# Plain tiles 2 and 3 written out in order with attention stages at points, w_out blocks kept, weight steps spaced wider

## The chip, the core and the metric

The kernel runs on one core of a Trainium2 chip. The metric is the device time of one execution in microseconds (us). A core has TensorE (matmuls; PE in the profile, with PEld for its weight loads), VectorE (DVE), ScalarE (ACT), GpSimd (POOL), SyncE (SP), which here issues all DMAs, and 16 DMA engines.

## What is computed

Attention with keys and values pooled over 8 positions, then a first FFN (leaky ReLU), then an RMS norm and a second FFN (gated by SiLU), in float32 (the weights come as float64 and are converted by bit operations):

```python
# q, k, v: (8, 8, 576, 64); 4608 tokens of 512 features
k_p = k.reshape(B, H, 72, 8, D).mean(axis=3); v_p = v.reshape(B, H, 72, 8, D).mean(axis=3)
scores = q @ k_p.T / sqrt(D)
attn = exp(scores - max(scores)); attn = attn / (attn.sum(-1) + 1e-09)
x = (attn @ v_p).transpose(0, 2, 1, 3).reshape(4608, 512)
h = x @ w_in                              # w_in 512 x 2048
x = maximum(0.01 * h, h) @ w_out          # w_out 2048 x 512
xn = x / sqrt(mean(x * x) + 1e-06) * rms_g
g = xn @ w_gate; val = xn @ w_val         # 512 x 1536 each
out = (g * sigmoid(g) * val) @ w_out2     # w_out2 1536 x 512
```

## The kernel before

**Numbers.** Every float32 operand is kept as two parts, HI and LO, and a product is three matmuls (`TERMS`): HI x HI, HI x LO, LO x HI. Splitting an operand takes a copy on ScalarE (the high part) and a subtraction on VectorE or GpSimd (the low part).

**Attention** goes by batch b (0 to 7) and by tiles t (0 to 4) of 128 queries. Steps of one tile: `t` transposes the queries (TensorE rows `qt`), `s` makes the scores in two halves (`sc`) and the softmax (VectorE maximum and subtraction, ScalarE exponential, VectorE sum, reciprocal, product), `x` transposes the result (`xt`, and a small rest `xr`) and splits it. Per batch, `kp` and `vp` pool keys and values on GpSimd, `kt` transposes the keys, and `av` multiplies with the values (`av0` after tile 1, `av1` after tile 4). The result goes to the token tiles `xhl` in SBUF, or from token 1536 on to `x_dram`.

**First FFN, plain tiles.** The first 1536 tokens are three plain tiles of 512 (`PLAIN` = 3; here tile 0, 1, 2). For each of 16 blocks f of the hidden layer, `h_unit` multiplies with a block of w_in (128 hidden units, 12 matmuls, rows `h`), ScalarE and VectorE make the activation's parts, and two blocks later `y_unit` multiplies with the block of w_out (12 matmuls into four banks, rows `y`). In tile 0 the first 8 blocks are done in halves of 256 columns, because its last 256 tokens come later. Attention's steps (`seq`) are cut by shares into lists for the three tiles (`by_tile`, `border`) and put between the units. This part is ordered by the compiler's scheduler, which simulates times; `own(...)` keeps some instructions in the order of the code.

**First FFN, pairs.** The other 3072 tokens are three pairs of tiles (pair 0, 1, 2), computed with seven block products instead of eight (`Quad`: p1 to p7, rows `xh`, `yh`, `wh` on operands `xa`, `T`, `xb`, `ah`). A pair has 8 quads; the second half z=1 of its output is multiplied afterwards with all 16 blocks of w_out again (`y_part`, rows `o<-ug,wo`). Its operands are written to DRAM by `operand_steps` in tile 2 (GpSimd rebuilds the weights, VectorE forms sums, ScalarE and GpSimd split them, SyncE stores them) and come back by `load_a` into ten slots; w_out comes back by `load_o` into four slots. `token_steps` forms the token sums T1 to T4 of a pair. From the first pair on every engine keeps the order of the code. After each product (a **point**) `tick` issues a part of what is left of attention (`late_attention`: query tiles from (4, 2) on, `RATE` = 7 points apart) and, when attention has ended, one step of `side_steps`, which prepares the second FFN's weights in the same way: per unit a load, a conversion, sums, split, store, with a unit every 6 (gate and value) or 4 points (w_out2).

**Second FFN.** Five more pairs with six g/v quads each; `norm_steps` computes their RMS norm in points of the pair before.

## Time and profile before

| | us |
|---|---|
| three runs | 1942.01, 1946.44, 1946.67 |
| median | 1946.44 |
| profiled execution, time | 1941.65 |
| profiled execution, span | 1939.9 |
| TensorE busy | 1782.7 |
| its weight loads busy | 1498.6 |
| VectorE, ScalarE, GpSimd busy | 967.2, 734.0, 697.4 |

The mean granted clock of TensorE is 0.963 of full speed. How to read the rows below: a row of the table of stretches has the stretch (us from the span's start), its length, the busy time and the count of instructions of each engine, then TensorE's granted clock (1.00 is 2.4 GHz, 0.50 is 1.2 GHz), the share of time in which the DMA engines were busy, and GB/s. A row of the timeline has start, length, engine, line, operation, output and inputs, size, and in brackets the idle time before it with what ended it; matmuls overlap, so the distance of two starts tells more than a length. A row of waits has who waited for whom, us in all, how often, and the longest. A row of groups has busy time and mean length.

### The profile page before, as it was taken

To read this page: it belongs to the slowest core of one execution; us is meant where nothing else is said; L and a number is where in the kernel's file an instruction comes from. 1 tells how busy PE (TensorE), PEld (TensorE's weight loads), DVE (VectorE), ACT (ScalarE), POOL (GpSimd) and SP (SyncE) were. 2 spreads that over 40 slices of the span, in tenths; PEclk is the share of its full clock that TensorE was granted. 3 is DMA by queue.
4 is the path that set the end of the run, shared out by engine and by line. 5 is a ranking of instruction groups with operands and counts; after the bars stand their busy time and mean duration, and the time that the engine had idled before them with its cause. 6 is when DMAs were issued, how large, how long until landed. Compare 5 with 4: busy or idle time off the path is not lost. (4 is left out here: it accounts for less than half of the span.)

```text
span 1939.9 us, 24263 instructions
## 1 busy us (share of the span) xinstructions
PE 1782.7 (92%) x8452; PEld 1498.6 (77%) x8452; DVE 967.2 (50%) x1622; ACT 734.0 (38%) x1566; POOL 697.4 (36%) x792
## 2 busy tenths in 40 slices
...
GB/s 266 303 158 100 26 74 58 93 311 256 206 207 224 233 126 300 345 348 253 334 269 342 186 246 195 209 233 291 252 270 210 195 230 275 249 274 205 194 206 103
DMA packets 222345, 429.43 MB, mean 221 GB/s; under 512 B 60176, under 2 KB 114448, under 8 KB 221712
## 3 DMA queue, kind: packets, MB, share of 16 engines
...
## 5 line engine op out<-in xcount | busy, mean ns | idle before, releaser
L1282 PE MATMUL o<-wo,u 128*128 128x512 f32 x1296 | 315.2, 391 | 2.8 <-DMA wo<-wo 2.7
L1282 PEld LDWEIGHTS o<-wo,u 128*128 128x128 f32 x1296 | 242.2, 188 | 52.2 <-DMA wo<-wo 4.3
L1262 PE MATMUL o<-ug,wo 128*128 128x512 f32 x576 | 150.7, 413 | 19.4 <-DMA wo<-wo 8.6
L665 PE MATMUL h<-xhl,w_i 128*128 128x512 f32 (+1 forms) x672 | 155.9, 380 | 2.3 <-ACT g L100 1.9
L701 PE MATMUL y<-ghl,w_o 128*128 128x256 f32 (+1 forms) x768 | 152.0, 343 | 3.0 <-ACT ye L714 1.8
L1262 PE MATMUL o<-u,wo 128*128 128x512 f32 x576 | 148.1, 396 | 0.0
L1262 PEld LDWEIGHTS o<-ug,wo 128*128 128x128 f32 x576 | 111.1, 198 | 47.1 <-ACT oe L1269 9.2
L97 POOL TENSOR_TENSOR u<-e2g,u 128x512 fp32r<-128x512 f32 (+1 forms) x25 | 29.5, 1182 | 310.6 <-ACT u L94 310.6
L665 PEld LDWEIGHTS h<-xhl,w_i 128*128 128x128 f32 x672 | 120.2, 201 | 23.5 <-ACT g L100 2.9
L701 PEld LDWEIGHTS y<-ghl,w_o 128*128 128x128 f32 x768 | 120.8, 191 | 18.5 <-ACT ye L714 2.1
L1262 PEld LDWEIGHTS o<-u,wo 128*128 128x128 f32 x576 | 107.8, 190 | 21.8
L1173 POOL TENSOR_TENSOR u<-gu,u 128x512 fp32r<-128x512 f32 x42 | 56.2, 1337 | 168.9 <-ACT gu L100 168.8
L1152 PE MATMUL xh<-xa,ah 128*128 128x512 f32 x288 | 78.3, 409 | 15.0 <-ACT e1h L1196 15.0
L1152 PE MATMUL yh<-T,ah 128*128 128x512 f32 x288 | 79.4, 413 | 7.0 <-DVE e6h L1127 4.7
L1152 PE MATMUL yg<-T,ag 128*128 128x512 f32 (+1 forms) x360 | 84.1, 369 | 0.0
L1152 PE MATMUL yv<-T,av 128*128 128x512 f32 (+1 forms) x360 | 83.9, 368 | 0.0
L1152 PE MATMUL xg<-xa,ag 128*128 128x512 f32 (+1 forms) x360 | 83.8, 368 | 0.0
L1152 PE MATMUL xv<-xa,av 128*128 128x512 f32 (+1 forms) x360 | 83.8, 368 | 0.0
L231 POOL TENSOR_TENSOR v<-v 128x256 f32<-128x256 f32 (+2 forms) x84 | 56.4, 675 | 57.8 <-DMA v<-in_v_dram 54.2
L1152 PEld LDWEIGHTS xh<-xa,ah 128*128 128x128 f32 x288 | 54.8, 195 | 27.3 <-ACT e1h L1196 16.5
L1152 PEld LDWEIGHTS yg<-T,ag 128*128 128x128 f32 x360 | 66.0, 188 | 9.9 <-DVE e1v L1127 0.6
L1152 PEld LDWEIGHTS yv<-T,av 128*128 128x128 f32 x360 | 66.2, 188 | 9.5
...
## 6 DMA issues: line engine op xcount, KB each, us to landing
...
```

The source lines that it names most:

```text
L97: lo_eng.tensor_tensor(out=lo, in0=src, in1=hi.bitcast(F32), op=ALU.subtract)
L231: nc.gpsimd.tensor_tensor(out=x[:, :n], in0=x[:, :n], in1=x[:, n:2 * n], op=ALU.add)
L665: nc.tensor.matmul(pt, w[:, sp, c * P:(c + 1) * P], x[:, mp, c, :], start=c == 0 and i == 0, stop=c == n_k - 1 and i == 2,)
L701: nc.tensor.matmul(pt, w[:, sp, m * P:(m + 1) * P], g[:, mp, a - c0:a - c0 + n], start=ydone[j, a] == 1 and i == 0 and m % per_bank == 0, ...
L1152: nc.tensor.matmul(pt, wt[:, a, c, sp, :], xt[:, mp, :], start=start and c == 0 and i == 0, stop=c == 1 and i == 2, skip_group_check=not s ...
L1173: eng.tensor_tensor(out=t[:, LO, :], in0=g, in1=t[:, HI, :].bitcast(F32), op=ALU.subtract)
L1262: nc.tensor.matmul(pt, w[:, sp, m * P:(m + 1) * P], u[:, mp, :], start=f == 0 and i == 0, stop=f == F1 - 1 and i == 2,)
L1282: nc.tensor.matmul(pt, u[:, sp, m * P:(m + 1) * P], w[:, mp, :], start=f == 0 and i == 0, stop=f == F2 - 1 and i == 2,)
```

## The change

- Attention's steps of batch 1 up to `av0` stay in plain tile 0, the others of batch 1 stand behind its last units but two (`border`). Batches 2 to 7 all go through `late_attention`, which now begins with plain tile 1: query tiles 7 points apart, 9 from point 57 on, 8 from point 124 on.
- Plain tiles 1 and 2 are written out in chunks of six matmuls (`h_half`, `y_unit` with two of four banks); after each chunk come the steps put at that point (stores of w_out in tile 1; operand steps at 15 + 5p and the first pair's loads and token steps at 42 to 61 in tile 2) and one attention point. Every engine keeps the order of the code from there on.
- The operand steps are cut in five, and two pairs of slots take turns (5, 7 and 9, 11).
- A unit of the second FFN's weights takes 8 points instead of 6, its parts stand further apart, and its load stands two points earlier.
- In the pairs, the last four w_out blocks of the first half are used first in the second half, and the first four of the next pair are used last there, without a load. The first two blocks of a second half and the last two of a first half are done bank pair by bank pair.
- Token steps are cut finer, and the norm's steps begin at quad 3 after their loads at quad 1.

```diff
-    FIRST_LATE = next(i for i, (b, t) in enumerate(tiles) if b * S + QT[t] >= PLAIN * N + 2 * N)
+    FIRST_LATE = next(i for i, (b, t) in enumerate(tiles) if b == 2)
     cut = seq.index(("s", *tiles[FIRST_LATE]))
     seq, late_seq = seq[:cut], seq[cut:]
...
-    RATE = 7
...
-        for n, i in enumerate(range(FIRST_LATE, len(tiles))):
+        s = -7
+        for i in range(FIRST_LATE, len(tiles)):
             b, t = tiles[i]
-            s = n * RATE
+            s += 7 if s < 57 else 9 if s < 124 else 8
             stage(("s", b, t), (s, s + 1, s + 2, s + 3))
             stage(("x", b, t), (s + 4, s + 5, s + 6))
...
+    def h_half(j, f, half):
+
+        if half == 0:
+            gp[j, f] = bank("h", 2, f"h{j}_{f}")
+        pt, w, x = gp[j, f], W1.done["i", f], xhl[j]
+        for c in (2 * half, 2 * half + 1):
+            for i, (sp, mp) in enumerate(TERMS):
+                nc.tensor.matmul(
+                    pt, w[:, sp, c * P:(c + 1) * P], x[:, mp, c, :],
+                    start=c == 0 and i == 0, stop=c == KC - 1 and i == 2,
+                )
+        if half:
+            h_parts(j, f, 0, pt)
...
+    def y_unit(j, f, c0, c1, ms=range(KC)):
...
-            ydone[j, a] += 1
-            for m in range(KC):
+            ydone[j, a] += ms[0] == 0
+            for m in ms:
...
+        def rebuilt():
+            r = held["r"] = per.tile([P, 2, 512], F32, tag="w1", bufs=1, name=f"r{p}")
+            for i, w in enumerate((w0, w1)):
+                nc.gpsimd.tensor_tensor(
+                    out=r[:, i, :], in0=w[:, HI, :].bitcast(F32), in1=w[:, LO, :].bitcast(F32), op=ALU.add
+                )
...
+        def high():
...
-                t = weight_slot(5 + 2 * i, f"hs{p}_{i}").rearrange("p h n -> p (h n)")
+                t = weight_slot(((5, 7) if p in (0, 1, 3, 5, 7) else (9, 11))[i], f"hs{p}_{i}")
...
+        def low():
+            for x, t, d in held["t"]:
+                nc.gpsimd.tensor_tensor(
                     out=d[:, :, LO, :], in0=x, in1=d[:, :, HI, :].bitcast(F32), op=ALU.subtract
-                ))
...
-        return [sums, parts, store]
+                )
+            ready.update([("h", p)] * 1)
+
+        return ((0, rebuilt), (2, sums), (4, high), (5, low), (7, store))
...
-            at(begin + 5, lambda: convert(held["raw"]))
+                    (nc.sync.dma_start(out=dst, in_=d.bitcast(F32).rearrange("p a h n -> p a (h n)")))
+
...
+            at(max(begin - lead, 0), start)
+            at(begin + 5, lambda: convert(held["raw"], 0))
+            at(begin + 6, lambda: convert(held["raw"], 1))
             if len(zs) == 2:
-                at(begin + 5, lambda: sums(
+                at(begin + 7, lambda: sums(
                     held["raw"].bitcast(F32).rearrange("p (k i n) w -> p k i n w", k=2, i=2)
                 ))
             for i, (z, t0) in enumerate(zs):
                 at(begin + t0, lambda i=i, z=z: high(i, z))
                 at(begin + t0 + 1, lambda i=i: low(i))
-                at(begin + t0 + 3, lambda i=i: store(i))
+                at(begin + t0 + 4, lambda i=i: store(i))
...
                     unit(
-                        begin, n, f"{m}{p}_{c}", lambda t: t.rearrange("p (k f) w -> p k (f w)", k=2),
+                        begin, 2, n, f"{m}{p}_{c}", lambda t: t.rearrange("p (k f) w -> p k (f w)", k=2),
                         src[:, p * 2 * W:(p + 1) * 2 * W].rearrange("(k c p) f -> c p k f", k=2, p=P)[c], srcs,
-                        ((0, 6), (1, 8)),
+                        ((0, 9), (1, 10)),
                     )
-                    begin += 6
+                    begin += 8
...
                 unit(
-                    begin, n, f"p{f}", lambda t: t.rearrange("p n w -> p (n w)"), rows(w_out2, f), srcs,
-                    ((f % 2, 7),),
+                    begin, 0, n, f"p{f}", lambda t: t.rearrange("p n w -> p (n w)"), rows(w_out2, f), srcs,
+                    ((f % 2, 8),),
                 )
                 begin += 4
...
-    free2 = [9, 11, 13, 15, 8, 10] + [12, 14, 17, 16, 18, 19, 20, 22, 21, 24] + [26, 23, 25, 27]
-    free2 += [0, 2, 4, 6, 28, 30, 29, 31, 1, 3, 5, 7]
+    free2 = [13, 15, 8, 10, 9, 11] + [12, 14, 17, 16, 18, 19, 21, 20, 22, 24] + [26, 23, 25, 27]
+    free2 += [28, 30, 0, 2, 29, 31, 4, 6, 1, 3, 5, 7]
...
-    o_todo = [(q, z, f) for q in range(len(pairs)) for z in range(2) for f in range(FS[kinds[q]])]
+    def blocks(q, z):
+        n = FS[kinds[q]]
+        return [*range(n - 4, n), *range(4, n - 4), *range(4)] if kinds[q] == 1 and z else [*range(n)]
+
+    def kept(q, z, f):
+
+        if kinds[q] == 2:
+            return None
+        if z == 0 and f >= F1 - 4:
+            return q, 1, f
+        return (q + 1, 0, f) if z == 1 and f < 4 and kinds[q + 1] == 1 else None
+
+    o_todo = [(q, z, f) for q in range(len(pairs)) for z in range(2) for f in blocks(q, z)]
+    for key in o_todo[:]:
+        if kept(*key):
+            o_todo.remove(kept(*key))
...
-        o_tiles[key] = t
+        while key:
+            o_tiles[key] = t
+            key = kept(*key)
...
-    def first_pair():
+    def first_pair(put):
 
         xs, loads = pair_loads(0)
-        early, late = token_steps(0, xs)
-        when = {10: loads}
-        for i, x in enumerate(early):
-            when.setdefault(12 + i, []).append(x)
-        for i in range(A_SLOTS):
-            when.setdefault(10 + i // 2, []).append(load_a)
-        for i in range(3):
-            when.setdefault(14 + i // 2, []).append(load_o)
-        return when, late
+        early, late = token_steps(0, xs, True)
+        for i, x in enumerate(loads):
+            put(44 + i, x)
+        for i, x in zip((42, 43, 45, 47, 48, 49, 51, 53, 55, 57), range(A_SLOTS)):
+            put(i, load_a)
+        for i in range(O_SLOTS):
+            put(57 + i // 2, load_o)
+        for i, x in zip((50, 51, 52, 53, 55, 56, 57, 58), early):
+            put(i, x)
+        for i, x in enumerate(late):
+            put(60 + i, x)
...
+    jobs = (
+        [(f, 0, CH[0][1]) for f in range(HALVES)] + [(f, 0, N) for f in range(HALVES, F1)]
+        + [(f, CH[0][1], N) for f in range(HALVES)]
+    )
...
+    def attention_slot():
+        for x in plan.pop(0) if plan else ():
+            run_step(x)
+
+    for i, (f, c0, c1) in enumerate(jobs):
+        h_unit(0, f, c0, c1)
+        attention_slot()
+        if i >= 2:
+            y_unit(0, *jobs[i - 2])
+        if W1.left():
+            W1.step()
+            W1.step()
...
+        attention_slot()
+    while plan:
+        attention_slot()
+    for x in border:
+        run_step(x)
+    y_unit(0, *jobs[-2])
+    y_unit(0, *jobs[-1])
+    assert not W1.left()
+    y_store(0)
+
+    late_attention()
+    late_end = max(at_point) + 1
+    begun = len(nc.cur_bb.bb.instructions)
+
+    for j in range(1, PLAIN):
+        at_spot = {}
+
+        def put(i, x):
+            at_spot.setdefault(i, []).append(x)
+
+        if j == 1:
+            for f in range(F1):
+                put(4 * f, lambda f=f: store_wo(f))
+        else:
+            for p in range(F1 // 2):
+                for i, x in operand_steps(p):
+                    put(15 + 5 * p + i, x)
+            first_pair(put)
+        chunks = []
+        for f in range(F1 + 2):
+            if f < F1:
+                chunks += [lambda f=f, half=half: h_half(j, f, half) for half in range(2)]
+            if f >= 2:
+                chunks += [lambda f=f, ms=ms: y_unit(j, f - 2, 0, N, ms) for ms in ((0, 1), (2, 3))]
+        for i, x in enumerate(chunks):
+            x()
+            for f in at_spot.pop(i, ()):
+                f()
+            attention_point()
+        assert not at_spot
...
-    def queue_out(q, z, f):
-        for ms in ((0, 1), tuple(range(2, pairs[q][1] // P))):
-            def one(ms=ms):
-                if ms[0] == 0:
+    def queue_out(q, z, fs):
+        groups = ((0, 1), tuple(range(2, pairs[q][1] // P)))
+        todo = [(f, ms) for f in fs for ms in groups]
+        if kinds[q] == 1 and (fs[0] == F1 - 2 or z):
+            todo[:4] = [(f, ms) for ms in groups for f in fs[:2]]
+        for f, ms in todo:
+            def one(f=f, ms=ms):
+                if ms[0] == 0 and (q, z) == (last_q, 1):
+                    load_a()
+                out_part(q, z, f, ms)
+                if ms[0] and not kept(q, z, f):
                     load_o()
-                    if (q, z) == (last_q, 1):
-                        load_a()
-                out_part(q, z, f, ms)
...
         def between():
+            if side:
+                tick()
             if norm and (i >= 2 or i == 1 and len(norm) > n_norm - 2):
...
             def spot():
-                if i >= 1 and norm:
+                if norm and (i >= 3 or i >= 1 and len(norm) > n_norm - 2):
                     norm.pop(0)()
...
             second_half(q, 1)
             for i in range(4):
                 piece()
                 tick()
-                if i % 2:
-                    second_half(q, 2 + i // 2)
+                if i > 1:
+                    second_half(q, i)
         while pieces:
...
         for i in range(len(pieces) - (4 if more else 0)):
             if kinds[q] == 1:
-                if loads and i % 4 == 0:
+                if loads and i in (0, 1, 4, 8):
                     loads.pop(0)()
-                if not loads and i >= (14 if kinds[q + 1] == 1 else 4) and i % 2 == 0 and early + late:
+                piece()
+                if early + late and (i >= 12 if kinds[q + 1] == 1 else i >= 4 and i % 2 == 0):
...
+                for k in (4, 5) if i == 3 else (i // 2 + 4,) if i % 2 and i > 3 else ():
+                    if k < F1:
+                        second_half(q, k)
                 tick()
                 continue
-            if side:
-                tick()
```

The order of instructions shows it in three places. In all of them a row is line, operation, output and inputs, size. TensorE, where plain tile 0 ends and tile 1 begins, before (`y_256_*` are products of tile 0's second half, `av_1_*` value products of batch 1, `h_0_0_2109` is tile 1's first block):

```order
L701 MATMUL y_256_1_1113<-ghl_6_256_1990,w_o_816 128x256
L405 MATMUL av_1_0_2036<-at_1_1670,vb_0_1097 128x320 x3
L410 MATMUL av_1_0_2036<-atr_1_1671,vb_4_1308 128x320
L405 MATMUL av_1_1_2046<-at_1_1670,vb_1_1150 128x320 x3
L410 MATMUL av_1_1_2046<-atr_1_1671,vb_4_1308 128x320
L701 MATMUL y_256_1_1113<-ghl_6_256_1990,w_o_816 128x256 x5
L701 MATMUL y_256_0_1112<-ghl_7_256_2020,w_o_871 128x256 x6
L701 MATMUL y_256_1_1113<-ghl_7_256_2020,w_o_871 128x256 x6
L665 MATMUL h_0_0_2109<-xhl_736,w_i_308 128x512
```

The same place after the change (`sc_2` are scores of query tile 2 of batch 1, `qt_3` and `xt_2` transposes, `kt_0` of batch 2's keys):

```order
L330 MATMUL sc_2_0_1859<-kblk_72,qT_2_1460 128x144 x2
L330 MATMUL sc_2_1_1864<-kblk_72,qT_2_1460 128x144 x2
L695 MATMUL y_256_0_1068<-ghl_6_256_1811,w_o_816 128x256 x6
L695 MATMUL y_256_1_1069<-ghl_6_256_1811,w_o_816 128x256 x6
L695 MATMUL y_256_0_1068<-ghl_7_256_1841,w_o_871 128x256 x6
L695 MATMUL y_256_1_1069<-ghl_7_256_1841,w_o_871 128x256 x6
L306 MATMUL qt_3_1874<-ident,q_3_1211 128x128 x4
L286 MATMUL kt_0_1904<-ident,kp_0_1883 128x128
L286 MATMUL kt_0_1904<-ident,kp_1_1890 128x128
L286 MATMUL kt_0_1904<-ident,kp_2_1897 128x128
L377 MATMUL xt_2_1921<-ident,ex_2_1857 128x128 x4
```

Two blocks of tile 0 are left behind the scores of query tile 2; scores and transposes of tiles 3 and 4 and the value products follow in the same way, with no product of the FFN between them, up to tile 1's first block 18 rows further down.

TensorE inside plain tile 2, before (`xt_3`, `sc_4`, `xt_4`, `av_1` belong to batch 3, `qt_0` to batch 4):

```order
L701 MATMUL y_0_0_3355<-ghl_5_0_3564,w_o_752 128x512
L701 MATMUL y_0_1_3356<-ghl_5_0_3564,w_o_752 128x512
L701 MATMUL y_0_2_3357<-ghl_5_0_3564,w_o_752 128x512
L701 MATMUL y_0_3_3358<-ghl_5_0_3564,w_o_752 128x512
L377 MATMUL xt_3_3422<-ident,ex_3_3338 128x128 x4
L383 MATMUL xr_3_3429<-ident,er_3_3419 96x128 x2
L330 MATMUL sc_4_0_3448<-kblk_72,qT_4_3376 128x144 x2
L330 MATMUL sc_4_1_3453<-kblk_72,qT_4_3376 128x144 x2
L306 MATMUL qt_0_3463<-ident,q_0_3268 128x128 x4
L377 MATMUL xt_4_3493<-ident,ex_4_3446 128x128 x4
L383 MATMUL xr_4_3500<-ident,er_4_3490 96x128 x2
L405 MATMUL av_1_0_3505<-at_1_3321,vb_0_2894 128x320 x3
```

TensorE at the same query tile of batch 3 after the change:

```order
L330 MATMUL sc_3_0_4052<-kblk_71,qT_3_3915 128x144 x2
L654 MATMUL h_10_4062<-xhl_2043,w_i_1015 128x512 x6
L330 MATMUL sc_3_1_4069<-kblk_71,qT_3_3915 128x144 x2
L654 MATMUL h_10_4062<-xhl_2043,w_i_1015 128x512 x6
L306 MATMUL qt_4_4097<-ident,q_4_3759 128x128 x4
L695 MATMUL y_0_0_3441<-ghl_8_0_3931,w_o_942 128x512 x3
L695 MATMUL y_0_1_3442<-ghl_8_0_3931,w_o_942 128x512 x3
L695 MATMUL y_0_2_3443<-ghl_8_0_3931,w_o_942 128x512 x3
L695 MATMUL y_0_3_3444<-ghl_8_0_3931,w_o_942 128x512 x3
L654 MATMUL h_11_4138<-xhl_2043,w_i_1091 128x512 x6
L377 MATMUL xt_3_4150<-ident,ex_3_4050 128x128 x4
L654 MATMUL h_11_4138<-xhl_2043,w_i_1091 128x512 x6
```

Before, transposes and scores of two query tiles stand in a row; after, six matmuls of the tile stand between any two of them.

ScalarE at the end of pair 1, before (`raw_g` converts a loaded weight of the second FFN, `parts_g` splits its sums, `u`, `gu` are the activation of a quad that TensorE waits for):

```order
L100 ACTIVATE u_1_14_7863<-xh_7_7826 128x512
L100 ACTIVATE gu_1_14_7862<-xh_7_7826 128x512
L100 ACTIVATE raw_g_0_7815<-raw_g_0_7815 128x512
L845 ACTIVATE parts_g_0_0_7885<-raw_g_0_7815 128x2x128 x2
L100 ACTIVATE u_2_15_7906<-e7h_7_7882 128x512
L845 ACTIVATE parts_g_0_1_7908<-raw_g_0_7815 128x2x128
L845 ACTIVATE parts_g_0_1_7908<-raw_g_0_7815 128x128
L100 ACTIVATE u_1_15_7919<-e1h_7_7833 128x512
L100 ACTIVATE gu_1_15_7918<-e1h_7_7833 128x512
```

ScalarE at the same place after the change:

```order
L848 ACTIVATE parts_p_1_7888<-raw_p_7795 128x512
L100 ACTIVATE raw_g_0_7822<-raw_g_0_7822 128x512
L100 ACTIVATE u_2_15_7871<-e6h_7_7817 128x512
L94 ACTIVATE ug_12_7924<-u_2_13_7741 128x512
L94 ACTIVATE ug_13_7927<-u_2_13_7741 128x512
L1309 COPY oe_0_1_7946<-o_0_1_7016 128x512
L848 ACTIVATE parts_g_0_0_7949<-raw_g_0_7822 128x2x128 x2
L848 ACTIVATE parts_g_0_1_7960<-raw_g_0_7822 128x2x128
L848 ACTIVATE parts_g_0_1_7960<-raw_g_0_7822 128x128
```

Between a conversion and the splits that need VectorE's sums of it there was nothing; now four instructions stand between.

## Rows read from the trace of the kernel before

**Rows 1.** Table of stretches: us, length, busy (x count) by engine, PEclk, DMA share, GB/s.

```profile
179.80:295.50 115.70, 107.47 (x514) 89.52 (x513) 50.98 (x98) 39.96 (x102) 36.66 (x70) 0.93 0.20 57
295.50:434.60 139.10, 121.50 (x539) 98.83 (x537) 60.45 (x115) 54.98 (x128) 49.29 (x52) 0.88 0.49 156
434.60:699.70 265.10, 228.65 (x1127) 184.76 (x1125) 153.29 (x277) 114.76 (x289) 109.06 (x159) 0.94 0.68 214
699.70:897.00 197.30, 177.30 (x749) 141.66 (x749) 92.61 (x161) 79.64 (x164) 73.42 (x78) 0.97 0.86 301
897.00:1108.00 211.00, 178.70 (x725) 142.73 (x724) 117.54 (x182) 92.27 (x183) 91.70 (x89) 0.91 0.83 285
1108.00:1939.90 831.90, 825.23 (x3857) 708.67 (x3855) 355.46 (x527) 251.08 (x439) 256.16 (x215) 1.00 0.67 224
```

**Rows 2.** Timeline of TensorE in tile 2: start, length, row, count.

```profile
414.64 2.88 PE L665 MATMUL h<-xhl,w_i 128*128 128x512 f32 x12
417.36 2.88 PE L701 MATMUL y<-ghl,w_o 128*128 128x512 f32 x12
```

**Rows 3.** Timeline of TensorE in pair 0.

```profile
477.89 0.66 PE L330 MATMUL sc<-kblk,qT 128*128 128x144 f32 x4
478.29 1.64 PE L1152 MATMUL yh<-T,ah 128*128 128x512 f32 x6
...
481.65 0.60 PE L306 MATMUL qt<-ident,q 128*128 128x128 f32 x4
482.00 1.64 PE L1152 MATMUL wh<-T,ah 128*128 128x512 f32 x6
```

**Rows 4.** Timeline of TensorE at the border inside tile 1.

```profile
245.93 1.15 PE L330 MATMUL sc<-kblk,qT 128*128 128x144 f32 x8
...
253.81 2.29 PE L330 MATMUL sc<-kblk,qT 128*128 128x144 f32 x8 [0.98 <-DVE at L97]
...
265.85 3.56 PE L665 MATMUL h<-xhl,w_i 128*128 128x512 f32 x12
```

**Rows 5.** Waits of TensorE, 434 to 700 us: total, times, longest.

```profile
PE sc L330 <- DVE at L97: 5.4, 1, 5.4
PE xt L377 <- DVE ex L347: 5.3, 8, 1.2
PE o L1262 <- DMA wo<-wo: 4.2, 2, 2.8
PE xh L1152 <- ACT e1h L1196: 4.2, 1, 4.2
```

**Rows 6.** Groups of GpSimd, 330 to 440 us: busy, mean ns, idle before.

```profile
L760 POOL TENSOR_TENSOR r<-w_i 128x512 f32<-128x512 f32 x12 | 17.0, 1438 | 11.2 <-DVE s L769 11.2
L779 POOL TENSOR_TENSOR hs<-s,hs 128x512 fp32r<-128x512 f32 x12 | 16.5, 1381 | 21.0 <-ACT hs L778 13.9 <-DMA op_h<-hs 7.1
```

**Rows 7.** Tile hs, idle time before its instructions by what ended it.

```profile
  DMA op_h<-hs: 14.2, 5
```

**Rows 8.** Waits of ScalarE, 640 to 1110 us.

```profile
ACT parts_g L845 <- DMA op_g<-parts_g: 14.1, 5, 4.6
...
ACT parts_g L845 <- DVE raw_g L823: 10.2, 4, 4.6
...
ACT acc L981 <- DMA xst<-y: 8.4, 1, 8.4
```

**Rows 9.** Waits of TensorE, pair 1.

```profile
PE wh L1152 <- ACT gu L100: 5.5, 4, 1.9
...
PE o L1262 <- ACT oe L1269: 3.9, 1, 3.9
```

**Rows 10.** Waits of TensorE, pair 2.

```profile
PE wh L1152 <- ACT gu L100: 12.6, 2, 7.4
PE xh L1152 <- ACT e1h L1196: 6.9, 1, 6.9
```

226 lines of the change are left out of this document (74 added, 152 removed).

## Prediction

> **What bounds the kernel now.** I read the table of stretches first, then the waits of TensorE in the stretches that lose time, then what the engines behind those waits did themselves.
>
> [rows 1] cut the span at the places where TensorE's work changes its kind: plain tile 1 (179.8 to 295.5 us), plain tile 2 (to 434.6), pair 0 (to 699.7), pair 1 (to 897.0), pair 2 (to 1108.0), second FFN (to the end). In the second FFN the clock is 1.00 and TensorE is busy for 825.2 of 831.9 us: nothing is left there. The five stretches ahead of it last 928 us, and there it idles and its clock is 0.88 to 0.97.
>
> What these five cost at full speed can be counted. Twelve 512-column matmuls start 2.72 us apart from the next twelve [rows 2], so one is 0.2267 us. A plain tile has 384 of them (16 blocks x 24): 87.0 us. A pair has 720 (8 quads x 7 products x 6, and 2 halves x 16 blocks x 12): 163.2 us. A tile of 128 queries costs two score groups of 0.40 us and two groups of four transposes of 0.35 us [rows 3], some 0.15 us for the two small transposes, and its share of the value products, priced by columns, and of the key transposes, 0.9 us: 2.6 us, an estimate. With 12 query tiles in plain tiles 1 and 2 and 18 in pair 0 (a little of it in pair 1), the lost time is:
> plain tiles 1 and 2: 254.8 - 174.1 - 31.2 = 49.5 us; pair 0: 265.1 - 163.2 - 46.8 = 55; pair 1: 197.3 - 163.2 - 2 = 32; pair 2: 211.0 - 164 = 47. Together 184 us. Idle time and the lower clock in [rows 1] give about the same (36.5 us idle in pair 0, 32.3 in pair 2). That is all the change can win, and it moves work only here.
>
> **The change part by part.** The sum is made against the profiled execution (span 1939.9, time 1941.65 us), 4.8 us under the median of 1946.44.
>
> *Border of tile 0 and tile 1: a new loss.* Before, query tiles 2 to 4 of batch 1 stand between the last blocks of tile 0, and tile 1 follows at 179.8 us with no gap. Now they stand behind them; the last 24 half-width matmuls (2.9 us) are all that covers them. Their work leaves tile 0: 3 x 1.65 us and 2.7 us of value products and key transposes, 7.7 us, so tile 0 ends at 172. Uncovered, one query tile is a chain of scores, softmax and transposes, 7.9 us from one tile's scores to the next's in the border that the old tile 1 has [rows 4]: 245.93 to 253.81; from the last scores to the first matmul of a tile it took 12.0 us (to 265.85). From the first of the three scores that is 7.9 + 7.9 + 12.0 = 28 us less some 2 us, since tile 1 needs only half of the value products to start. It begins at 172 - 2.9 + 26 = 195 us: **+15 us**.
>
> *Plain tiles 1 and 2.* The two old borders inside them (246 to 266 us, and two more in tile 2) go: now one attention step in turn stands behind each group of six matmuls, 7 points per query tile up to point 57, then 9, later 8. It is what pair 0 had already, with 7. There the row on transposes waiting for softmax has 5.3 us in 8 waits [rows 5], and with the other small ones some 0.75 us per query tile are lost; the plain tile asks less of VectorE and ScalarE per point than a quad does. 16 query tiles now fall into these two tiles: 174.1 + 16 x 2.6 + 16 x 0.75 = 227.7 us. In tile 2 come eight operand steps, five points apart (8.3 us with attention's share): each has two sums of 1.44 us and two differences of 1.38 us on GpSimd [rows 6], 5.6 us of 8.3, beside the pooling of keys and values. As the order is fixed now, a late sum holds VectorE, and that holds softmax. The price is bounded by nothing (GpSimd keeps up) and by 8 x 2.8 us (each step late by its two sums); I take 13, nearer the upper end since GpSimd is nearly full there, and 2 us for slow matmuls behind the border. Stage 243 us instead of 254.8: **-12 us**.
>
> *End of tile 2.* The first pair's loads, sums and splits stand at points 42 to 61. The operand tiles' write-backs already hold up their own buffers: 14.2 us in 5 waits [rows 7]. Splitting them over two pairs of slots takes that away, but slots 9 and 11 also hold T3 of the first pair: its split on ScalarE, at point 55, must wait for the store issued at point 52. The Trainium skill ("DMA: Bandwidth & Descriptors", Queues, rings and completion order) says that each DMA engine takes its descriptors in ring order; by that the store leaves behind all loads issued before it, and the split waits. What it would cost is the third rival; in the sum it has 0 to 10 us, and I take 3, within the 28 us of pair 0.
>
> *Pair 0.* 14 query tiles instead of 18: 163.2 + 36.4 = 199.6 us. Before, its start waited for ScalarE and for the token sums, 4.2 us for one copy [rows 5], and lost some 19 us with the lower clock; the sums are now finished three points or more ahead, and I leave 9 (with the 3 from above). Middle and second half: 14 x 0.75 = 10.5 us; the second half's waits for softmax (5.4 us once) and for w_out blocks (4.2 us) [rows 5] shrink with 8 points per tile and with four blocks that are still in their slots; 8 left. 227 us with half a microsecond to spare, instead of 265.1: **-37.5 us**.
>
> *Pair 1 and pair 2, the spacing of the second FFN's weights.* ScalarE works in program order. It stood waiting for its own weight pieces: for the write-back of the piece before (14.1 us in one row alone), for VectorE's sums that were issued in the same point (10.2 us), and once for the normalisation's input (8.4 us) [rows 8]. Behind it stood the copies that TensorE waits for: 5.5 us in pair 1 [rows 9], 12.6 and 6.9 us in pair 2 [rows 10]. Now a unit has 8 points instead of 6, its sums stand two points ahead of the split, its store has four points instead of three before the slot is used again, and the normalisation starts two quads after its loads instead of at once: the 8.4 us go, and with them most of the 7 us wait they caused. The first four blocks of the second half and of the next pair come without a load, 20 of 96 loads. The last two blocks are done bank by bank, which gives each bank 2.7 us more to be emptied; that answers the 3.9 us for the output copy [rows 9]. From both sides: nothing gained if the DMA engines, not the spacing, are the limit (0.86 and 0.83 busy [rows 1]); all 79 us if no wait stays. Term by term I leave half: 17 of 32 in pair 1, 27 of 47 in pair 2: **-17 and -20 us** (163.2 + 17 and 164 + 27, against 197.3 and 211).
>
> *Queues the moved steps pass.* On SyncE a weight's load is issued two points earlier and, for every sixth unit, ahead of the point where its slot is read last; it holds the operand loads behind it for three points (some 5 us). These are ten slots ahead of their use, 2.5 quads or 40 us: nothing. The steps need 249 points and 240 are left in the pairs, so nine spill into the second FFN, where the other engines are half idle [rows 1]: **+1 us**.
>
> Sum: 15 - 12 - 37.5 - 17 - 20 + 1 = -70.5 us, 1871 us against the profiled run; the median lay above its profiled run, so I put it at **1874 us**.
>
> **The rivals.**
> 1. *The pairs are bound by the DMA engines, so their waits stay.* For it: 0.86 and 0.83 busy over whole stretches, and ScalarE's longest waits are for stores. Against: the waits for VectorE, for the normalisation's input and for the output copy are no matter of bandwidth, and the weights' traffic is spread over a quarter more time. Pairs 1 and 2 keep all but 8 us of what they lose: 1874 + 37 - 8 = 1903 us.
> 2. *The other side: strict order turns every query tile in the plain tiles into a border.* If VectorE or GpSimd lag by more than the two points between softmax and transposes, each tile costs what an uncovered one does: 7.9 us for 1.65 us of TensorE's work, 6.2 us lost instead of 0.75. That is 16 x 5.5 = 88 us: 1962 us, slower than before. It decides from 5.2 us per tile (0.75 + 70.5 / 16). For it: one order for all, GpSimd full in tile 2. Against it: pair 0 ran this very scheme with 0.75 us, and plain tiles leave ten points between a block's first and second product.
> 3. *The jam at the end of tile 2*, by ring order. Points 42 to 57 ask for four loads of tokens, ten of operands and the stores of four steps, more than that stretch can move; the store that T3 waits for comes last. ScalarE would stand from point 55 for some six points, 10 us, and softmax with it; with the lower clock behind it and a start of pair 0 as late as before (10 us more): 1874 + 20 = 1894 us. The Trainium skill's rule named above would make it so; the 14.2 us of [rows 7] show such waits at a third of that length each.
> 4. *More is won*: all five stretches lose only what the middle of pair 0 loses, 10 us each in the pairs' ends gone: 1874 - 40 = 1834 us.
>
> **How the numbers follow.** Forecast 0.48; rival 1, 0.19; rival 3, 0.15; rival 4, 0.08; rival 2, 0.10. The range must leave out no more than two in ten: it leaves out rival 2 and the far half of rival 4, and takes in the forecast's own spread and rivals 1 and 3 together (1923): 1840 to 1928 us. A measurement of this kernel tells some 0.3% from no change, 5.8 us: faster than 1940.6 us in all cases but rival 2 and a small rest of the first; 0.85 faster, 0.05 within, 0.10 slower.
>
> **What would show it.** A profile of the changed kernel should show the first full-width matmul of tile 1 near 195 us after a stretch of low clock; no stretch of four or more waiting transposes in a row in tiles 1 and 2, and their 768 matmuls done by 438 us; pair 0 starting with less than 5 us of waiting; no wait of ScalarE for the normalisation's input; waits for w_out blocks under 2 us a pair; pair 2 done before 1045 us. I am wrong if tile 1 begins past 205 us, if GpSimd's sums are waited for in tile 2 for more than 25 us, or if pairs 1 and 2 still take 195 us and more.

## The result: 1916.2 us, where 1874 was forecast

The changed kernel takes 1916.24 us (median; 1911.88 to 1918.14) and the kernel before, on the same chip, 1944.76 (1942.01 to 1946.67): a ratio of 0.9851, 95% interval 0.9828 to 0.9874. The gain is 28.5 us; 70.5 were forecast. The sign and the range held, the size did not. The profiled execution took 1915.0 us, its span 1913.2. Its table of stretches, cut as [rows 1] were (after tile 0 with the border: tile 1, tile 2, pair 0, pair 1, pair 2, second FFN; columns as there):

```profile
0.00:197.09 197.09, 145.62 (x928) 131.69 (x929) 131.43 (x257) 99.80 (x255) 69.00 (x111) 0.85 0.49 154
197.09:322.45 125.36, 120.00 (x617) 99.17 (x617) 65.22 (x133) 53.52 (x146) 45.27 (x88) 0.99 0.40 128
322.45:469.39 146.94, 121.11 (x570) 98.58 (x569) 88.38 (x147) 60.15 (x143) 79.78 (x89) 0.92 0.64 209
469.39:702.73 233.34, 209.49 (x1045) 171.62 (x1044) 126.14 (x229) 99.54 (x247) 83.80 (x124) 0.97 0.61 193
702.73:879.67 176.94, 167.81 (x722) 135.53 (x721) 88.98 (x146) 74.64 (x151) 71.87 (x73) 0.99 0.87 297
879.67:1070.52 190.85, 174.01 (x726) 139.07 (x724) 117.30 (x179) 89.56 (x181) 92.87 (x88) 0.96 0.83 289
1070.52:1913.20 842.68, 829.11 (x3857) 711.16 (x3855) 361.70 (x534) 254.24 (x446) 262.87 (x221) 0.99 0.65 225
```

Against the forecast sum (span 1939.9 - 70.5 = 1869.4):

| stretch | before | forecast | after | error |
|---|---|---|---|---|
| tile 1 begins at | 174.4 | 195 | 197.1 | +2 |
| plain tiles 1 and 2 | 260.2 | 243 | 272.3 | **+29** |
| pair 0 | 265.1 | 227.6 | 233.3 | +6 |
| pair 1 | 197.3 | 180.3 | 176.9 | -3 |
| pair 2 | 211.0 | 191 | 190.9 | 0 |
| second FFN | 831.9 | 832.9 | 842.7 | **+10** |

The prediction has 179.8 us for the first row before, and 254.8 us from there to the end of tile 2; but tile 1's first full-width block stands earlier, at 174.40 us (the timeline of TensorE, before):

```profile
174.40 2.92 PE L665 MATMUL h<-xhl,w_i 128*128 128x512 f32 x12
```

So up to the end of tile 2 the change loses 34.8 us (434.6, then 469.4), and pairs 0, 1 and 2 win 31.8, 20.4 and 20.2.

Tile 2 is where most of the error lies. The longest of TensorE's waits there, and below them the longest of pair 0, at its start (total, times, longest):

```profile
PE xt L377 <- DVE ex L347: 13.8, 6, 4.8
PE av L405 <- ACT xs L421: 9.3, 1, 9.3
```

```profile
PE xh L1191 <- ACT e1h L1235: 9.1, 1, 9.1
```

What ScalarE, behind which the two long ones stand, waited for from 322 to 500 us:

```profile
ACT ye L708 <- DMA y<-ye: 17.4, 2, 12.9
...
ACT g L100 <- DMA x<-xs: 9.2, 1, 9.2
```

Neither is the wait that the third rival named (the split of T3 behind the store of an operand tile). `xs` (results of the attention), `g`, `ye` (results of the tile) and the first pair's token sums share three buffers (tag `tg`); a copy into one must wait until the write-back of an older one has landed. SyncE's own rows show why the xs of 434.52 us is freed so late (start, length of the issue):

```profile
432.05 1.44 SPq L786 DMA_DIRECT2D op_h<-hs  x2
433.57 0.66 SPq L788 DMA_DIRECT2D op_h<-w_i  x1
434.28 1.61 SPq L792 DMA_DIRECT2D op_h<-w_i  x1
435.93 1.02 SPq L788 DMA_DIRECT2D op_h<-w_i  x1
437.19 2.93 SPq L792 DMA_DIRECT2D op_h<-w_i  x1
440.22 0.42 SPq L422 DMA_DIRECT2D x<-xs  x1
```

Six write-backs of one operand step (1.75 MB) stand ahead of it; the issues of the four copies take 0.7 to 2.9 us each, where the medians of the two lines are 0.53 and 0.76, while the DMA engines are 1.00 busy (432 to 440 us). The copy is done at 434.95 us, issued at 440.22 and landed at some 445.7: 5.3 us on SyncE and 5.4 in the queue. The waits of the transposes (13.8 us) have another cause, and the longest of them is to be read on two engines. VectorE, then GpSimd:

```profile
361.75 0.74 DVE L344 TENSOR_REDUCE st<-ex 128x8 f32<-128x576 f32 x1
362.53 4.99 DVE L345 TENSOR_SCALAR st<-st 128x8 f32<-128x8 f32 x1
```

```profile
362.55 2.51 POOL L780 TENSOR_TENSOR hs<-s,hs 128x512 fp32r<-128x512 f32 x2
365.01 2.48 POOL L753 TENSOR_TENSOR r<-w_i 128x512 f32<-128x512 f32 x2
```

An addition over 128x8, 0.17 us elsewhere (median of 40), stands for 4.99 us and ends when the fourth of these GpSimd instructions does. There were thus two theories for tile 2: G, the operand steps' arithmetic holds softmax (by GpSimd or by VectorE's own order); Q, the write-backs hold the small results.

### The profile page after: what moved, and what is told of

Its sections match the earlier page's. It is cut to its first block, busy times and chain, and to the rows that moved or that the text cites. A ratio compares the mean times of both kernels' runs of the same rounds, so it can differ in the third digit from the quotient of the medians.

```text
span 1913.2 us, 24286 instructions
## 1 busy us (share of the span) xinstructions
PE 1767.2 (92%) x8452; PEld 1486.8 (78%) x8452; DVE 979.1 (51%) x1622; ACT 731.4 (38%) x1566; POOL 705.5 (37%) x792
## 4 chain that ended last, share of the span: by engine, by line
PE 55%; DMA 9%; DVE 6%; ACT 3%; POOL 2%; issue 2%; SPq 1%; ACTq 0%; POOLq 0%; DVEq 0%
PE o L1322 15%; PE yg L1191 6%; PE yv L1191 6%; PE o L1302 5%; PE wv L1191 4%; PE wg L1191 4%; PE xv L1191 4%; PE xg L1191 4%; PE yh L1191 3%; DMA op_v<-parts_v 2%; PE xh L1191 2%; DMA op_g<-parts_g 2%; PE wh L1191 2%; DMA wo<-parts_p 1%; DMA q<-in_q_dram 1%
## 5 line engine op out<-in xcount | busy, mean ns | idle before, releaser
L1302 PE MATMUL o<-ug,wo 128*128 128x512 f32 x576 | 142.5, 400 | 10.4 <-ACT oe L1309 6.7
L654 PE MATMUL h<-xhl,w_i 128*128 128x512 f32 x384 | 104.9, 415 | 0.0
L654 PEld LDWEIGHTS h<-xhl,w_i 128*128 128x128 f32 x384 | 72.2, 197 | 13.3
L672 DVE TENSOR_TENSOR ghl<-g,ghl 128x512 fp32r<-128x512 f32 (+1 forms) x56 | 40.2, 717 | 77.1 <-ACT g L100 76.8
L1191 PEld LDWEIGHTS yg<-T,ag 128*128 128x128 f32 x360 | 66.0, 188 | 10.2 <-DVE e1v L1166 0.6
L1191 PEld LDWEIGHTS xv<-xa,av 128*128 128x128 f32 x360 | 66.0, 188 | 9.6
```

Of the source, the lines that this page charges most:

```text
L654: nc.tensor.matmul(pt, w[:, sp, c * P:(c + 1) * P], x[:, mp, c, :], start=c == 0 and i == 0, stop=c == KC - 1 and i == 2,)
L672: nc.vector.tensor_tensor(out=t[:, LO, :], in0=g, in1=t[:, HI, :].bitcast(F32), op=ALU.subtract)
L1191: nc.tensor.matmul(pt, wt[:, a, c, sp, :], xt[:, mp, :], start=start and c == 0 and i == 0, stop=c == 1 and i == 2, skip_group_check=not s ...
L1302: nc.tensor.matmul(pt, w[:, sp, m * P:(m + 1) * P], u[:, mp, :], start=f == blocks(q, z)[0] and i == 0, stop=f == blocks(q, z)[-1] and i == 2,
```

## The experiments

Every ratio is against the kernel before on the same chip; unless a base is named, the edit is made in the changed kernel (1916.2 us, 0.9851; 0.9828 to 0.9874). Differences in us are between medians taken on different chips; by the ratios each comes out the same within 2.5 us, and where two intervals overlap the difference is not clear of noise.

**The border undone.**

```diff
-    mine, border = seq[:final], seq[final:]
+    mine, border = seq, []
```

> Changed kernel, but the steps of batch 1 that stand in a row behind tile 0's last blocks are spread over tile 0's attention slots with the others. Theory: the border costs what the prediction put on it, 15 us; tile 1's first full-width matmul comes at 180 to 184 us instead of 197.1, and the time falls by 12 to 17 us, to 1899 to 1904. Rival: softmax and weight conversion fill VectorE and ScalarE in tile 0, tile 0 becomes as much longer, tile 1 begins later than 190 and the time stays within 5 us of 1916.

1899.67 us, 0.9769 (0.9751 to 0.9787): 16.6 us less. Tile 1 begins at 186.6 us, later than either 180 or 184, so 10.5 us of it are the border itself; of the rest the profile has 3.2 in tile 1, 2.3 in tile 2 and 2.2 in the second FFN. Steps that stood uncovered are covered by tile 0's blocks. Tile 1 still begins 12.2 us later than before the change (174.4), which the border does not explain.

**Copies written back in tile 1** (the four of six write-backs that copy weights).

```diff
...
+            for p in range(F1 // 2):
+                put(8 * p + 6, operand_steps(p, early=True))
```

> Changed kernel, but the four of the six write-backs of each operand step that copy input weights unchanged (0.75 MB of 1.75 MB a step, 6.3 MB in all) are issued in plain tile 1, so that tile 2 has only the write-backs of computed tiles. Theory Q (queue): the two long stalls at the end of tile 2 (TensorE 9.3 us at 447.7 behind ScalarE's wait for the write-back of xs, and 9.1 us at 482.0 behind its wait for the write-back of ye) come from small results waiting in a full queue; both fall under 3 us and the time falls by 10 to 18 us from the changed kernel's 1916, to 1898 to 1906. Theory G (GpSimd): the operand steps' arithmetic holds softmax, the queue is filled by the loads of the first pair anyway; the two stalls stay over 6 us each, the waits of transposes for softmax in tile 2 stay near 13.8 us, and the time stays within 4 us of 1916.

1905.95 us, 0.9796 (0.9766 to 0.9826): 10.3 us less, in the band of Q. The stall on `xs` falls from 9.3 to 3.4 us, the one on `e1h` only from 9.1 to 6.3; the transposes' waits stay (12.6 us). Tile 2 takes 140.2 us, pair 0 230.0. Q is right on part of the loss, and on neither of the two stalls entirely.

**Four operand loads behind the tile's results.**

```diff
-        for i, x in zip((42, 43, 45, 47, 48, 49, 51, 53, 55, 57), range(A_SLOTS)):
+        for i, x in zip((44, 46, 48, 51, 54, 57), range(6)):
             put(i, load_a)
+        for i in (130, 132, 134, 136):
+            at_point.setdefault(i, []).append(load_a)
```

> Changed kernel, but of the ten first operand loads (0.5 MB each) only six are issued in tile 2, the other four at points 2 to 8 of pair 0, behind the write-backs of tile 2's result. Theory Q (queue): the wait for the write-back of ye at pair 0's start falls from 12.9 us on ScalarE to under 6 and TensorE's 9.1 us with it; 5 to 10 us gained, 1906 to 1911. Theory G (GpSimd): no change beyond 4 us. A third way: the loads are then late for quad 1 or 2, pair 0 waits for ah and loses 3 to 8 us.

1916.68 us, 0.9855 (0.9834 to 0.9876): nothing. Tile 2 is 3.0 us shorter (the `xs` stall 4.1 us), ScalarE still waits 11.5 us for `ye` (TensorE 7.8), and pair 1 comes out 4 us longer. The forecast of Q failed here.

**Small results on ScalarE's queue.**

```diff
-                nc.sync.dma_start(out=x_dram[j][:, p, t0 - j * N:t1 - j * N], in_=x)
+                nc.scalar.dma_start(out=x_dram[j][:, p, t0 - j * N:t1 - j * N], in_=x)
```

and the same for `ye`.

> Changed kernel, but the write-backs of attention results (xs) and of the plain tiles' results (ye) are issued by ScalarE instead of SyncE. Theory R (order: they wait behind what SyncE issued before them, in its program and in its queue): the 9.2 us wait of ScalarE for xs and the 12.9 us one for ye fall under 4 us, TensorE's two long stalls (9.3 and 9.1 us) under 3, and the time by 12 to 20 us, to 1896 to 1904. Theory B (bandwidth: the 16 DMA engines are 0.99 busy there, so it comes as late from any queue): the waits stay over 7 us each, the time within 4 us of 1916.

1921.69 us, 0.9878 (0.9858 to 0.9899): 5 us more, outside both bands, though the intervals overlap. ScalarE's wait for `ye` falls from 12.9 to 3.7 us at the longest, as R has it, and TensorE's 9.1 to 5.0; but now ScalarE stands 5.8 us behind the operand write-backs as well, the `xs` stall is 10.8 us and tile 2 152.8. Order and the full queue both matter, and a second issuer did not help here, with the same bytes to move.

**The sums r on VectorE.**

```diff
-                nc.gpsimd.tensor_tensor(
+                nc.vector.tensor_tensor(
                     out=r[:, i, :], in0=w[:, HI, :].bitcast(F32), in1=w[:, LO, :].bitcast(F32), op=ALU.add
```

> Changed kernel, but the two sums r of each operand step (16 in all, 1.3 us each on GpSimd) run on VectorE (0.7 us each). Theory G (GpSimd): its arithmetic beside VectorE's softmax is what makes the transposes of tile 2 wait (13.8 us in 6 waits, one of them 4.85 us behind a 128x8 instruction that took 4.99 us instead of 0.17); with half of it gone these waits fall under 6 us and the time by 8 to 15 us, to 1901 to 1908. Theory Q (queue): the long stalls at the end of tile 2 stay; the transposes' waits fall by half at most, VectorE has 11 us more to do, and the time stays within 4 us of 1916.

1911.49 us, 0.9832 (0.9812 to 0.9852): 4.7 us less, between the two bands and not clear of noise (the intervals overlap). The waits for softmax hardly fall (12.5 us). The hold moved: the two sums, now on VectorE, take 4.18 us there while GpSimd's `hs` runs. VectorE's timeline of that run:

```profile
362.55 4.18 DVE L753 TENSOR_TENSOR r<-w_i 128x512 f32<-128x512 f32 x2
366.65 0.74 DVE L344 TENSOR_REDUCE st<-ex 128x8 f32<-128x576 f32 x1
```

**The held instruction taken out** (the addition of 1e-9 to the denominators).

```diff
-        nc.vector.tensor_scalar(out=st[:, 1, :], in0=st[:, 1, :], scalar1=1e-9, scalar2=None, op0=ALU.add)
```

> Changed kernel without the addition of 1e-9 to the softmax denominators (a 128x8 instruction on VectorE for each query tile; the denominators are at least 1). That instruction took 5.00 us instead of 0.17 in tile 2, exactly until GpSimd's run of four instructions was over. Theory H (only this form of instruction is held off by GpSimd): the 4.85 us wait of the transposes falls under 1.5 us and tile 2 by 4 to 6 us, the time to 1910 to 1913. Theory V (any VectorE instruction that reads SBUF is held off): the reciprocal or the multiplication behind it takes the 4 to 5 us instead, and the time stays within 2 us of 1916.

1907.43 us, 0.9801 (0.9782 to 0.982): 8.8 us less, outside what both theories gave. For the mechanism V is right: the multiplication two instructions behind it takes 5.35 us (0.76 elsewhere), and tile 2 stays at 145.7. VectorE's timeline:

```profile
357.02 5.35 DVE L346 TENSOR_TENSOR ex<-ex,st 128x576 f32<-128x576 f32 x1
```

The gain is elsewhere: tile 1 begins 3.4 us earlier, tile 1 and pair 0 are some 1.5 us shorter each, second FFN 2.0. Why a 0.17 us instruction is worth that much in tile 0 was not looked into.

**The operand steps without arithmetic, without write-backs, with neither.** In the first, the operand tiles are copies of the weights, written at the old points; in the second the arithmetic stays and the tiles are written in tile 1 from the weights; in the third only the latter is left.

```diff
...
-        return ((0, rebuilt), (2, sums), (4, high), (5, low), (7, store))
+        return ((7, store),)
```

and, for the second and third, in the function that writes the copies back in tile 1:

```diff
...
+            for i, t in enumerate((w0, w1)):
+                nc.sync.dma_start(out=y[:, 1 + i].rearrange("p a c n -> p (a c n)"), in_=t.rearrange("p h n -> p (h n)").bitcast(F32))
```

> Changed kernel; the eight operand steps of tile 2 leave out their sums, differences and splits (the operand tiles hold copies of the weights instead, so the numbers of pair 0 to 2 are others) and keep all six write-backs at their points. Tile 2 lasted 146.9 us with 13.8 us of transposes waiting for softmax and a 9.3 us stall. Theory G (arithmetic): the waits for softmax fall under 5 us and tile 2 to 128 to 133. Theory Q (queue): tile 2 stays over 138 and the stalls of 9 us stay.

> Changed kernel; the operand steps keep their arithmetic, but nothing of them is written back in tile 2: all operand tiles are written in tile 1 from the weights (so the numbers of the pairs are others). Theory Q: both 9 us stalls vanish (under 2 us each), tile 2 falls to 130 to 135 and pair 0 by 5 to 10 from 233.3. Theory G: tile 2 stays over 140.

> Changed kernel with neither: no operand steps in tile 2 at all, their tiles written in tile 1 from the weights. If the two causes add, tile 2 takes 125.4 us less two query tiles of 3.4 us, plus 3 us for the first pair's loads and sums: 119 to 124 us. If it stays over 130, a third cause is left (the first pair's own steps, the order of softmax behind the blocks' activations).

They took 1900.85 us (0.9772, 0.9755 to 0.9789), 1905.21 (0.9803, 0.9785 to 0.982) and 1879.06 (0.9665, 0.9651 to 0.9679). Tile 2 in each of the three, from its table of stretches:

```profile
324.60:455.00 130.40, 114.09 (x568) 94.63 (x567) 62.48 (x115) 51.11 (x127) 35.13 (x57) 0.95 0.71 234
```

```profile
324.20:469.00 144.80, 123.39 (x569) 100.09 (x568) 90.39 (x148) 60.09 (x143) 79.83 (x90) 0.92 0.40 126
```

```profile
323.80:443.20 119.40, 111.95 (x570) 92.95 (x569) 63.24 (x115) 51.11 (x127) 35.12 (x57) 1.00 0.48 149
```

| | write-backs in tile 2 | none |
|---|---|---|
| arithmetic | 146.9 | 144.8 |
| none | 130.4 | 119.4 |

With neither, tile 2 runs at full clock and loses 7 us. Arithmetic alone adds 25.4 us, write-backs alone 11.0, both 27.5: they do not add. That a tile slowed by one has time for the other is a reading of these four numbers, no more. Both theories were half right: without write-backs the long stalls shrink to 3.4 and 2.4 us, as Q said, but tile 2 stays at 144.8, as G said; without arithmetic the waits for softmax in tile 2 fall from 13.8 to 4.4 us, while stalls of 11.2 and 9.8 us stay. Pair 0 is 7.5 us shorter without the write-backs (225.8), and as long as ever without the arithmetic (233.9). In all, the operand steps cost 37 us (1916.2 - 1879.1), 27.5 of them in tile 2 and 5.8 in pair 0. Tile 2's 119.4 us lie in the band of the sum of both causes, so a third one is not needed there.

**Kept blocks and spacing.** Two parts of the change undone, one at a time: w_out blocks loaded again in pairs 1 and 2, and the weight steps with their old spacing.

```diff
-        if kinds[q] == 2:
+        if kinds[q] == 2 or q >= 1:
             return None
```

```diff
-            at(begin + 6, lambda: convert(held["raw"], 1))
+            at(begin + 5, lambda: convert(held["raw"], 1))
...
-                at(begin + 7, lambda: sums(
+                at(begin + 5, lambda: sums(
...
-                at(begin + t0 + 4, lambda i=i: store(i))
+                at(begin + t0 + 3, lambda i=i: store(i))
...
-                        begin, 2, n, f"{m}{p}_{c}", lambda t: t.rearrange("p (k f) w -> p k (f w)", k=2),
+                        begin, 0, n, f"{m}{p}_{c}", lambda t: t.rearrange("p (k f) w -> p k (f w)", k=2),
...
-                        ((0, 9), (1, 10)),
+                        ((0, 6), (1, 8)),
...
-                    begin += 8
+                    begin += 6
...
```

> Changed kernel, but in pairs 1 and 2 every w_out block is loaded for each half again (12 loads of 0.5 MB more). Theory S (spacing of the weight steps is what shortened pairs 1 and 2 from 408.3 to 367.8 us): they last at most 3 us longer. Theory K (the blocks kept in their slots did it, since the DMA engines are 0.83 to 0.87 busy there): 8 to 15 us longer, with waits of TensorE for w_out blocks of 5 us or more.

> Changed kernel, but the second FFN's weight steps have their old spacing and places (6 points a unit, conversion and sums in one point, splits 1 and 3 points behind, the load not ahead). Theory S (spacing): pairs 1 and 2 together last 380 to 390 us instead of 367.8, with ScalarE waiting 20 us or more for its pieces' write-backs and for VectorE's sums; nothing spills into the second FFN, which falls from 842.7 to 833; the time is 1919 to 1929. Theory K (kept blocks): pairs 1 and 2 stay under 372 us, the second FFN falls all the same, and the time is 1905 to 1910.

1930.08 us (0.9915, 0.9893 to 0.9937) and 1927.35 (0.9909, 0.9884 to 0.9934). Pairs 1 and 2, 367.8 us in the changed kernel, take 380.1 and 391.3. TensorE waits for w_out blocks in the first, for VectorE and ScalarE in the second:

```profile
PE o L1302 <- DMA wo<-wo: 10.9, 5, 4.2
```

```profile
PE yh L1191 <- DVE e6h L1166: 14.6, 5, 10.1
PE wh L1191 <- ACT gu L100: 9.1, 5, 2.7
```

So K and S are both true: 12.3 us are the kept blocks', 23.5 the spacing's; before was 408.3, 40.5 above the changed kernel, so 4.7 are left to the other edits or to both together. Second FFN under the old spacing: 831.3 us. The nine points of steps that spill into it cost 11.4.

**The spill taken away by a closer spacing.**

```diff
-                    begin += 8
+                    begin += 8 if p < 3 else 7
```

> Changed kernel, but the gate and value units of the last three pairs of weight blocks have 7 points instead of 8, so that the weight steps end with pair 2 (237 points for 240) and none spills into the second FFN. If the spill is what lengthened the second FFN by 10 us (TensorE's 5.7 us wait behind ScalarE's 10.2 us wait for a write-back at its start, and the low clock behind it), the second FFN falls to 831 to 834 us, pairs 1 and 2 grow by 0 to 4 us, and the time is 1906 to 1911. If it is something else at the start of the second FFN (its own table load or the last token steps), the second FFN stays over 838 us and the time at 1914 to 1920.

1949.77 us, 1.0036 (1.0021 to 1.0051): 0.4% slower than the kernel before, and outside both bands. The second FFN does fall to 833.6 us, but pair 2 takes 232.8 instead of 190.9, for one point of eight. Waits of ScalarE in pair 2, in the changed kernel and here:

```profile
ACT parts_g L848 <- DMA wo<-parts_p: 14.1, 4, 4.4
...
ACT parts_p L848 <- DMA op_v<-parts_v: 11.7, 2, 8.8
```

```profile
ACT parts_p L848 <- DMA op_v<-parts_v: 27.2, 6, 8.6
ACT parts_v L848 <- DMA op_g<-parts_g: 20.9, 5, 11.2
ACT parts_g L848 <- DMA op_g<-parts_g: 18.5, 5, 9.0
ACT parts_g L848 <- DMA wo<-parts_p: 17.3, 5, 6.9
```

and SyncE's there, at the loads of raw weights (L838) ahead of everything else it issues:

```profile
SPq L838 <- POOL parts_p L852: 24.6, 6, 7.4
SPq L838 <- POOL parts_v L852: 17.7, 4, 6.7
SPq L838 <- ACT parts_g L848: 17.6, 3, 8.7
SPq L838 <- POOL parts_g L852: 17.1, 5, 4.7
```

where the changed kernel has at these loads

```profile
SPq L838 <- POOL parts_p L852: 20.4, 6, 6.4
SPq L838 <- POOL parts_v L852: 9.6, 3, 4.6
```

The load of a unit stands two points ahead of its begin, in the slot that the unit before last must have been split from: at 8 points it is three points behind that unit's last split, at 7 only one. SyncE then waits for GpSimd, GpSimd for ScalarE, ScalarE for a write-back, and write-backs stand behind the waiting load on SyncE; the DMA engines' share falls from 0.83 to 0.72 while everything waits. That ring of waits is read from these rows; a run with the load alone moved was not made.

**The edits together.** Base of the first: no border, copies early, 7 points at the end, and the tile's results in two buffers that are free there. The second leaves out the addition too, the third also has r on VectorE. The fourth is the third with 8 points again. The edit that was not shown yet is in the store of tile 2's result:

```diff
-                t = per.tile([P, N], F32, tag="tg", bufs=3, name=f"ye{j}_{a}_{m}")
+                if m % 2 == 0:
+                    two = per.tile([P, 2, N], F32, tag="ghl", bufs=3, name=f"ye{j}_{a}_{m}")
+                t = two[:, m % 2, :]
```

> Changed kernel with four edits: no border (batch 1 spread over tile 0), copies of the operand steps written back in tile 1, last weight units at 7 points, and the four result tiles of tile 2 held in two buffers that are free there, so that ScalarE's copy of the last one does not wait for a write-back. If the losses are separate, the gains add: 16.6 (border) + 10.3 (copies) + 8 (spill) + 5 (pair 0's start) = 40 us, 1872 to 1882. If pair 0's start waits for the first operands or for the token tiles anyway, the last term is nothing: 1880 to 1888.

> As the run with four edits, and without the addition of 1e-9. Alone it gave 9 us, 4 of them ahead of tile 1, where the border has three query tiles in a row. Without the border these 4 are hidden and the gain is 3 to 6 us; if the addition costs in every query tile, it is 8 to 10 us again.

> As the run before, and with the sums r of the operand steps on VectorE. Alone it gave 4.7 us. If GpSimd's load in tile 2 still holds VectorE there, 3 to 6 us again; if VectorE is now what the end of tile 2 waits for, 0 to 4 us slower.

> No border, copies of the operand steps in tile 1, result tiles of tile 2 in two free buffers, no addition of 1e-9, sums r on VectorE; weight steps as in the changed kernel (8 points). The run with 7 points at the end lost 42 us in pair 2 and won 9 in the second FFN; without that edit 1904.4 - 33.5 = 1871, 1866 to 1876 us. If pair 2's 234 us in the runs with four edits had another cause as well, over 1880.

1917.58 (0.9876, 0.9847 to 0.9904), 1913.50 (0.9857, 0.9834 to 0.9881), 1904.36 (0.981, 0.979 to 0.983) and 1878.17 us (0.9658, 0.9643 to 0.9673). The first three carry the 42 us of the closer spacing in pair 2 (233.3, 234.3, 234.0 us); with 8 points pair 2 is 191.7. That took the first 35 us over its band. The addition is worth 4.1 us here, in its band but not clear of noise; r is worth 9.1 (4.7 alone), more than either theory gave it; and pair 0 falls to 225.4. The fourth is 2 us over its band.

**Two edits on that version.** GpSimd rid of the operand steps' last differences as well (on VectorE); and the weight steps begun some five points earlier, at the end of pair 0.

```diff
     def tick():
         attention_point()
+        if att is not None and point_now[0] >= late_end:
+            begin_phase2()
```

> As the best run so far (1878.2), with the last differences of the operand steps on VectorE too, so that GpSimd has only the pooling of keys and values in tile 2. If GpSimd's long runs of two-input sums are what holds VectorE there, the waits of transposes for softmax (10.6 us) halve and tile 2 falls from 132.7 to 122 to 128 us, the time to 1868 to 1874. If it is the number of instructions ahead of softmax on VectorE, whichever engine they were on, tile 2 stays within 3 us or grows, and the time is 1876 to 1884.

> As the best run so far (1878.2), with the weight steps of the second FFN begun some five points earlier, at the end of pair 0 as soon as attention is done, still 8 points a unit. If the spill of nine points is what costs 9 to 10 us at the second FFN's start, half of them or more come back: second FFN 832 to 838 instead of 841.9, the time 1868 to 1875. If the stall there is that of the last unit, however late it stands, nothing is gained: 1876 to 1880.

The first: 1880.41 us (0.9673, 0.965 to 0.9696), no gain. GpSimd's busy time in tile 2 falls from 61.5 to 38.7 us and the stage does not move (132.6, then 134.3). The row of tile 2 in that run:

```profile
308.80:443.10 134.30, 118.93 (x571) 97.37 (x569) 95.00 (x172) 60.42 (x144) 38.65 (x57) 0.95 0.56 187
```

GpSimd's hold is real for a single instruction, but it is not what the rest of the arithmetic costs; VectorE is busy for 95 us there against 63 without the steps, in one fixed order with softmax. Whether VectorE's order or ScalarE's splits ahead of its copies is the larger part stays open.

The second: **1868.68 us**, 0.9618 (0.9597 to 0.9639), the fastest run, 47.5 us under the changed kernel (45 by the ratios); it leaves out the addition of 1e-9. The second FFN is back at 831.2 us and pair 2 falls to 184.1; pair 1, which has more of the steps now, is 7 longer (184.4). Pair 0 is 5.4 us shorter (220.0) and tile 2, which the edit does not touch, 3.7 longer (136.4), so single stages differ by some us from profile to profile. Its row for the second FFN:

```profile
1032.80:1864.00 831.20, 824.79 (x3857) 708.49 (x3855) 356.90 (x529) 251.56 (x440) 258.13 (x217) 1.00 0.65 226
```

## Why the prediction was right in kind and wrong in size

Three terms of the sum failed: the price of a query tile, the price of the operand steps, and the spill. A fourth, time lost in tile 0 itself, was put at nothing and hidden by a misread row.

*Border, +15: right about the border, and the start of tile 1 in part by luck.* Score groups stand at 170.76, 179.07 and 187.05 us and tile 1's first block at 197.09 (forecast 195): 8.3, 8.0 and 10.0 us, where [rows 4] gave 7.9, 7.9 and 12.0. Undoing it gave 16.6 us back. But the 195 was counted from 179.8 us, where tile 1 began at 174.40; the same 927 recorded matmuls stand ahead of it before and after, and they take 22.7 us more. Some 11 us of that are there without the border too (186.6 us, with eight more value products ahead). They are lost in tile 0, mostly from 80 to 120 us; the row of that stretch before, and after the change:

```profile
80.00:120.00 40.00, 37.39 (x229) 33.46 (x228) 34.20 (x65) 25.28 (x62) 20.32 (x26) 0.96 0.66 216
```

```profile
80.00:120.00 40.00, 31.72 (x164) 26.72 (x163) 33.66 (x73) 26.30 (x65) 16.45 (x21) 0.82 0.47 140
```

TensorE has 164 matmuls in it instead of 229. No run looks into the cause, and the fastest kernel still has the loss (its tile 1 begins at 186.4 us).

*A query tile costs 2.6 us: the first step that failed.* Tile 1 has 120.0 us of busy TensorE at a clock of 0.99, 87.0 of them the tile's; 33 us go to nine tiles' transposes and 9.5 tiles' scores, 3.5 us each. The small matmuls themselves were priced well: they take 25 us, 2.7 a tile, value products and key transposes with them (a group of four value products 0.59 us, from 435.70 to 436.29):

```profile
435.70 0.60 PE L405 MATMUL av<-at,vb 128*128 128x320 f32 x3
...
436.29 0.66 PE L330 MATMUL sc<-kblk,qT 128*128 128x144 f32 x4
```

The other 8 us stand in the FFN's own matmuls, which the price left out. Six of 512 columns between two attention pieces take 1.49 us to the next start, in tile 1:

```profile
202.07 1.65 PE L654 MATMUL h<-xhl,w_i 128*128 128x512 f32 x6
203.56 0.65 PE L330 MATMUL sc<-kblk,qT 128*128 128x144 f32 x4
```

Six in a row without attention take 1.36, as counted; in pair 1:

```profile
742.17 1.52 PE L1191 MATMUL yh<-xb,ah 128*128 128x512 f32 x6
743.53 1.52 PE L1302 MATMUL o<-u,wo 128*128 128x512 f32 x6
```

The granted clock is 1.00 at both places. Tile 1 has 53 such groups, each some 0.15 us longer than counted; the first matmul of a group takes most of it (0.32 us to the next start, the median of 50, against 0.23). What on the chip makes it so, no run shows. The kernel before has it in pair 0 as well, where [rows 3] could have shown it: the `yh` at 478.29 us is followed 1.48 us later by

```profile
479.77 0.65 PE L330 MATMUL sc<-kblk,qT 128*128 128x144 f32 x4
```

There it was work that the prediction counted as waiting. In the plain tiles the new order brings most of it: 92 groups of large matmuls between attention pieces in tiles 1 and 2, where there were 37. Whether longer groups win some of it back was not tried. In all it is 14 us of the error in the plain tiles (16 tiles at 0.9) and 10 in pair 0 (209.5 - 163.2 us of busy TensorE for 14 tiles, 3.3 each). Pair 0's waits came out 4 us smaller than forecast, which hides part of that.

*Operand steps, 13 us between 0 and 22: the second.* The bound was GpSimd's two sums a step. They cost 27.5 us in tile 2, 25.4 by the arithmetic alone, above the upper bound, and 5.8 to 7.5 more in pair 0 by their write-backs. The prediction looked at the engine with the longest busy time; relieved of the sums r, that engine gave back 4.7 us (9.1 on the version without the border), and of the differences too, nothing. Its own sign to look for, VectorE waiting for GpSimd's sums, shows 1.8 us in tile 2. What remains, as far as the runs show, is the fixed order: the steps' instructions stand ahead of softmax and of the copies, and with the stalls comes the lower clock, 0.92 in tile 2 against 1.00 without the steps. Which engine's order weighs more is open.

*End of tile 2, 3 us; third rival, 0.15:* the rival's place and cause were right (small results behind bulk in the queue), its victim was not. Two stalls of 9 us came, through the `tg` buffers that the prediction never asked about, and pair 0 began with a 9.1 us wait where under 5 was promised. The Trainium skill ("DMA: Bandwidth & Descriptors", Queues, rings and completion order) says that each DMA engine consumes the descriptors of a ring in ring order; the trace agrees for the 5.4 us that `xs` spent behind operand tiles, but as much (5.3) was lost on SyncE before it was issued.

*Pairs 1 and 2, -17 and -20:* right: -20.4 and -20.2 us. ScalarE's wait for the normalisation's input [rows 8] is gone, waits for w_out are 2.1 and 0.6 us. The two sizes were half of what these pairs lost, a guess that came out, and not sums of priced waits. The first rival (bound by the DMA engines, 0.19) falls: their share is 0.87 and 0.83, as in [rows 1], and the pairs are 40 us shorter. Kept blocks and spacing share it as 12.3 to 23.5.

*Spill, +1: the third failed step,* 10.8 us by the profile (831.9, then 842.7) and 11.4 by the old spacing; started earlier, the steps left the second FFN at 831.2. "The other engines are half idle" was true and beside the point: ScalarE, in order, stood 10.2 us for a write-back with the first gate's activation behind it, and TensorE 5.7.

ScalarE's row and TensorE's, from their timelines:

```profile
1082.83 0.66 ACT L848 ACTIVATE parts_p<-raw_p 128x512 fp32r<-128x512 f32 x1 [10.16 <-DMA op_v<-parts_v]
```

```profile
1086.07 2.93 PE L1191 MATMUL yg<-xb,ag 128*128 128x512 f32 x6 [5.69 <-DVE e7g L1166]
```

The second rival (every tile a border) fell: tile 1, with nine query tiles in strict order, waits 5.4 us in all.

Sum of the error: 24 (price of a query tile) + 14.5 (operand steps) + 10 (spill) + 2 (start of tile 1) = 50.5, less some 7 for pair 0's waits and pair 1; the table has 44.

Of the prediction's signs, the plain tiles were done at 469 us instead of 438 and pair 2 at 1070.5 instead of 1045. None of its three "I am wrong if" came, so it had no sign for steps that cost time without being waited for.
